# Tiles that begin at byte 128 of a 256-byte line, later state halves and a newly planned order, in an attention and feed-forward kernel

## The chip, the cores and the metric

The kernel runs on one core of a Trainium2 chip. The metric is the device time of one launch in microseconds, taken as the median of three runs. The engines are named as in the profile: PE multiplies matrices, DVE is the vector engine, ACT the scalar engine, POOL the third elementwise engine, SP a queue that only issues DMAs here.

## The reference

`x` holds 8 batches of 8 heads with 512 rows of 64 numbers, `state` 32 rows for each batch and head. The rows of `x` attend to the state, the state's rows attend to `x`, both results are put together to 544 rows of 512 numbers for each batch, and a feed-forward layer with a squared ReLU follows (512 to 2048 to 512).

```python
scores  = scale * x @ state^T;  a  = softmax(scores)    # 512 x 32 for each head
xread   = a @ state
scores2 = scale * state @ x^T;  a2 = softmax(scores2)   # 32 x 512 for each head
sread   = a2 @ x
rows = concat(xread, sread)                             # 544 rows of 512 for each batch
h = rows @ w_in;  r = maximum(h, 0);  out = (r * r) @ w_out
```

## The kernel before

**Precision.** Results have to be as good as fp32, while fp32r operands keep fewer bits. So every operand of the large products is split into a high and a low part (`split`, L379): ACT casts the high part (L384), and DVE or POOL subtracts it from the value for the low part (L389). A product is then three matmuls: high by high, low by high, high by low.

**Products.** The matrix `state · w_in`, called z, is computed once for each group of four batches. For the first four batches `z_part` (L537) computes it while the weights come in, stores it to DRAM (`zd`), and `z_fetch` loads it again batch by batch (`z_raw`), which is then split to `z_hi` and `z_lo`. For the later four, `z_halves` (L461) loads the state's halves into `st_raw`, splits them into `st_hi` (ACT) and `st_lo` (POOL), `w_halves` splits pieces of `w_in` (`wz`) and `z_heads` (L500) multiplies the two.

**Units.** The feed-forward part consists of 144 units: for each of 8 batches and each of 16 chunks of 128 columns of `w_in`, and 16 more for the state's rows. A unit is "up" (L879: six matmuls of 128x512 into `ph`, from `a` and z), ReLU on ACT (L885), a square on DVE or ACT (L893, L891), the split of the result into `g_hi` and `g_lo`, and "down" (L915: twelve matmuls into four `po` banks, from `g_hi`, `g_lo` and the `w_out` chunk's `wo_hi`, `wo_lo`). The batch 0 is done in two parts, chunks 0 to 5, and 6 to 15 after batch 1.

**Weights.** They arrive as 64-bit words. `singles` makes fp32 of a chunk: a guard multiply on ACT (L402), the top bits on DVE (L411) or ACT (L409), and two DVE operations (L416, L422). For `w_out` the result `wof` is then split into `wo_hi` and `wo_lo`.

**Attention.** `scores` computes the score products of a batch and head group and their exponentials `e`; `read` (L784) normalizes them (`e` times `s`, L797), transposes them on PE (`pt`, L802), splits them into `e_hl` (ACT, DVE), splits the rows of `x` into `xn_hl` (ACT, POOL), and multiplies (`pr`, L820). `both` (L833) sums the parts up, and POOL places them (L846).

**What sets the order.** Nothing is scheduled by hand. The class `Planner` (L47 to L257) simulates the engines with a cost for each operation (`pe`, `act`, `dve`, `dve2`, `gps`, L260 to L277) and picks for the engine that is free first the ready operation that is due first. A due time comes from the unit an operation serves, and the table `SHIFTS` moves it for the nth tile of a name. The flag `both` marks a DVE operation that the plan reckons as if it ran only after the POOL operation in progress. While the plan has nothing for PE at the start, it puts small matmuls there (`keep_busy`, L937: four matmuls `idle` each). The planned order is then the order of the instructions of each engine; a queue runs its own in that order. `FIRST` and `STEP` (L325) are the planned lengths of the first and of the later units.

`Buf` (L20) makes the tiles when the plan is known. SBUF tiles of one tag lie side by side, in the order in which the tags first occur; so a small tag moves all that lie behind it.

Of the kernel before, what the change touches and what calls it, by code (L numbers as in the profile page):

```python
# [19 lines left out]
class Buf:  # L20


    def __init__(self, pool, shape, dtype, name, tag, bufs, hot=False):
        self.make = lambda: pool.tile(shape, dtype, name=name, tag=tag, bufs=bufs)
        self.tag, self.bufs, self.hot = tag, bufs, hot
        self.name = name.rstrip("0123456789")
        self.t, self.users = None, []
# [19 lines left out]
class Planner:  # L47
# [5 lines left out]
    SLACKS = (2.5,)  # L53
    EARLY = 150.0
    SHIFTS = {
        ("g_lo", 1): (-9.6, 0.0),
        ("nm", 1): (7.3, -0.01),
        ("nm", 2): (6.9, 0.0),
        ("pa", 1): (9.8, -0.29),
        ("ph", 2): (-1.4, 0.38),  # L60
        ("po", 1): (-3.2, 0.28),
        ("po", 5): (8.2, 0.0),
        ("po", 8): (-2.0, 0.0),
        ("po", 14): (-4.0, 0.0),
        ("po", 17): (8.9, 0.18),
        ("po", 19): (-6.0, 0.02),
        ("pr", 1): (3.6, 0.0),
        ("pz", 1): (-3.2, 0.0),
        ("s", 2): (-3.3, 0.3),
        ("spill", 1): (-6.6, 0.0),  # L70
        ("wi", 1): (3.9, 0.0),
        ("wo", 1): (2.7, 0.0),
        ("wof", 1): (12.4, -0.2),
        ("z_hi", 1): (7.7, 0.0),
    }

    def __init__(self):
# [89 lines left out]
    def plan(self, scale):  # L167
        for o in self.ops:
            o.due, o.begin = self.time(o.want), self.time(o.start)
            o.left, o.ready, o.end = o.before, 0.0, None  # L170
        for o in reversed(self.ops):
            cost = o.engs[0][1] + o.lat + scale * o.slack + (o.size / self.RATE + o.land if o.size else 0.0)
            for s_ in o.succ:
                o.due = min(o.due, s_.due - cost)
            if o.next is not None:
                o.due = min(o.due, o.next.due)
            if o.hold is not None:
                o.begin = max(o.begin, o.due - o.hold)
        for o in self.ops:
            if o.due < self.EARLY and o.kind in self.SHIFTS:  # L180
                more, slope = self.SHIFTS[o.kind]
                o.due += more + slope * max(o.due, -30.0)
        free, slots, pending, wait, taken, cands = {}, {}, {}, {}, set(), {}
        queue = pool_end = 0.0
        for o in self.ops:
            for k in o.bufs:
                pending[k] = len(k.users)
                slots.setdefault(k.tag, [0.0] * k.bufs)

        def offer(o):  # L190
            for e, _ in o.engs:
                cands.setdefault(e, {})[o] = None

        for o in self.ops:
            if not o.left:
                offer(o)
        log = []
        left = sum(o.until > 1e17 for o in self.ops)
        while left:
            best = self.choose(cands, free, slots, taken, True) or self.choose(cands, free, slots, taken, False)  # L200
            assert best is not None, "no operation can begin"
            t, e, o = best
            cost = dict(o.engs)[e]
            for f, _ in o.engs:
                del cands[f][o]
            for k in o.bufs:
                if k not in taken:
                    slots[k.tag].remove(min(slots[k.tag]))
                    taken.add(k)
                    if k.hot:  # L210
                        for u in k.users:
                            u.due = min(u.due, t + 2.0)
            end = t + cost
            if e == "POOL":
                pool_end = end
            elif o.both and e == "DVE":
                end = max(end, pool_end + cost)
            free[e] = end
            if o.size:
                queue = max(queue, end) + o.size / self.RATE  # L220
                o.end = queue + o.land
            else:
                o.end = end + o.lat
            log.append((t, end, e, o))
            left -= o.until > 1e17
            for k in o.bufs:
                pending[k] -= 1
                wait[k] = max(wait.get(k, 0.0), o.end)
                if not pending[k]:
                    slots[k.tag].append(wait[k])  # L230
            for s_ in o.succ:
                s_.left -= 1
                s_.ready = max(s_.ready, end if e == "PE" == s_.engs[0][0] else o.end)
                if not s_.left:
                    offer(s_)
            if o.next is not None:
                o.next.left -= 1
                o.next.ready = max(o.next.ready, t)
                if not o.next.left:
                    offer(o.next)  # L240
        return log
# [22 lines left out]
def act(n, more=0.0):  # L264
    return ("ACT", 0.05 + more + n / 1200)
# [8 lines left out]


def gps(n):
    return ("POOL", 0.15 + n / 450)  # L277


@with_exitstack  # L280
def memory_attention_then_relu2_ffn(
# [40 lines left out]
    WARM = 88  # L322
    COLD = 8
    PARTS = [(0, 0, 6), (1, 0, NFC), (0, 6, NFC)] + [(b, 0, NFC) for b in (*range(2, B - 1), B, B - 1)]
    START, FIRST, STEP = 8.0, (3.5,), 4.4  # L325

    const = ctx.enter_context(tc.tile_pool(name="const", bufs=1))
    sb = ctx.enter_context(tc.tile_pool(name="sb", bufs=2))
# [64 lines left out]
    def singles(out_f, words, r, w):  # L393
# [5 lines left out]
        n = 512  # L399
        high_r, low_r = [(k, 1) for k in r], [(k, 0) for k in r]  # L400
        op(
            act(n, 0.08), lambda e: nc.scalar.activation(  # L402
                high().bitcast(F32), high().bitcast(F32), AF.Copy, scale=GUARD),
            r=high_r, w=high_r,
        )
# [5 lines left out]
                nc.vector.tensor_scalar(  # L411
                    out=bits(), in0=top(), scalar1=1 / 32, scalar2=-15.5 / 32, op0=ALU.mult, op1=ALU.add)

        op([dve(n), act(n, 0.08)], top_bits, r=low_r, w=w)
        op(
            dve(n), lambda e: nc.vector.scalar_tensor_tensor(  # L416
                out=bits(), in0=high(), scalar=3, in1=bits(),
# [43 lines left out]
    def z_halves():  # L461

        raw = tile_([P, H, GB * N], F32, "st_raw", "raw")
        high, low = (tile_([P, H, GB * N], F32R, n, "raw") for n in ("st_hi", "st_lo"))
        src = stT.rearrange("d (h b n) -> d h b n", h=H, b=B)[:, :, GB:, :]
        flat = lambda t, j: t.t.rearrange("p h m -> p (h m)")[:, j * S:(j + 1) * S]
        for i in range(2):
            load(
                lambda i=i: raw.t[i * D:(i + 1) * D].rearrange("d h (b n) -> d h b n", b=GB),
                lambda: src, 256, w=[(raw, i)], issue=1.0,  # L470
            )
        for j in range(2):
            split(
                lambda j=j: flat(high, j), lambda j=j: flat(low, j), lambda j=j: flat(raw, j), S,
                [(raw, i) for i in range(2)], [(high, j)], [(low, j)], engs=[gps(S)], chain="w1",
            )
        halves[:] = [high, low]
# [306 lines left out]
    def read(b, g, due, begin=0.0):  # L784
# [9 lines left out]
            nc.vector.reciprocal(s2.t, s2.t)  # L794

        op(("DVE", 0.3), invert, r=[s2], w=[s2], begin=begin)
        op(dve2(S), lambda e: nc.vector.tensor_scalar_mul(e2.t, e2.t, s2.t), r=[e2, s2], w=[e2])  # L797
        pt = tile_([P, NT, P], F32, "pt", "px")

        def turn(e):  # L800
# [48 lines left out]
                        in1=low.t[i * N:(i + 1) * N, q, i * D:(i + 1) * D],  # L849
                    )  # L850

        op(("POOL", 1.5), place, r=[both, low], w=[("sr", b, g)], due=due)


    def wo_tile(fc):
# [294 lines left out]
```

## Time and profile before

| | before |
|---|---|
| median of 3 runs | 683.01 us (682.32 to 683.97) |
| the profiled execution | 685.25 us, span 683.5 us |
[...]
| PE busy | 673.6 us (99%) |
| DVE, ACT, POOL busy | 433.7, 411.2 and 166.4 us |
| DMA | 79.80 MB, mean 117 GB/s |

The table of busy times says how much of the span each engine worked. A row of the timeline gives the start, the length, the engine, the line, the operation and its tiles; in brackets stands how long the engine had been idle before it, and what ended that. An operation's length overlaps the next one's start by up to a tenth of a microsecond, and a matmul's by more.

### The profile page before, as it was taken

How to read it: one execution, taken by the hardware profiler on the slowest of the kernel's cores; microseconds unless marked ns; L12 is line 12 of the kernel's file. 1: busy time of each engine (PE TensorE's matmuls, PEld its weight loads, DVE VectorE, ACT ScalarE, POOL GpSimd, SP SyncE). 2: the span in 40 equal slices, each digit the busy share in tenths (PEclk: the TensorE clock that was granted, in tenths of full speed). 3: DMA queues.
4: the chain of work that ended last, by engine and by line, in shares of the span. 5: the costliest groups of instructions: out<-in, count | busy, mean ns of one | idle time of the engine just before them, and what ended most of it. 6: DMA issues, size and time to landing. Idle time of an engine off the chain costs nothing.

```text
span 683.5 us, 9676 instructions
## 1 busy us (share of the span) xinstructions
PE 673.6 (99%) x3260; PEld 544.5 (80%) x3260; DVE 433.7 (63%) x717; ACT 411.2 (60%) x782; POOL 166.4 (24%) x183
## 2 busy tenths in 40 slices
PE   8999998999999999999999999999999999999997
PEld 7777776888888877888888888888888788988886
DVE  6999988457574588553954486347746855543333
ACT  5999776465486688576843584357656654443331
POOL 1010005114152354134500451035244640000000
PEclk9999999999999999999999999999999999999999
DMA  9998983231152343334221322113222201012101
GB/s 311 340 321 271 322 283 135 93 127 63 32 185 112 119 144 110 140 116 133 77 96 32 97 88 98 31 66 106 95 91 93 77 17 63 1 31 62 32 0 61
DMA packets 51681, 79.80 MB, mean 117 GB/s; under 512 B 7088, under 2 KB 34096, under 8 KB 51632
## 3 DMA queue, kind: packets, MB, share of 16 engines
q1 hardware_dynamic: 46544, 61.76, 27.6%
q10 hardware_dynamic: 5088, 17.44, 6.5%
q8 instruction: 25, 0.41, 0.2%
q14 instruction: 24, 0.20, 0.1%
HBM read 52.43 MB, written 26.74 MB: 116 GB/s over the span
## 4 chain that ended last, share of the span: by engine, by line
PE 79%; ACT 6%; DVE 6%; DMA 5%; issue 2%; POOL 1%; SPq 1%; ACTq 0%; DVEq 0%; POOLq 0%
PE po L915 46%; PE ph L879 25%; PE pr L820 2%; PE pz L500 2%; DMA w_raw<-w_in 2%; PE pq L690 1%; DMA z_raw<-zd 1%; DMA wo_raw<-w_out 1%; ACT z_stage L520 1%; PE pt L802 1%; DVE z_lo L389 1%; PE idle L942 1%; PE pz L537 1%; DMA zd<-z_stage 1%; DVE g_lo L389 1%
## 5 line engine op out<-in xcount | busy, mean ns | idle before, releaser
L915 PE MATMUL po<-wo_hi,g_hi 128*128 128x512 f32 x544 | 215.1, 395 | 0.0
L915 PE MATMUL po<-wo_lo,g_hi 128*128 128x512 f32 x544 | 213.2, 392 | 0.0
L885 ACT ACTIVATE r<-ph 128x512 f32<-128x512 f32 (+1 forms) x144 | 82.7, 574 | 159.9 <-PE ph L879 157.7
L893 DVE TENSOR_TENSOR ph<-ph,r 128x512 f32<-128x512 f32 (+1 forms) x120 | 79.6, 664 | 147.2 <-ACT r L885 146.9
L915 PE MATMUL po<-wo_hi,g_lo 128*128 128x512 f32 x544 | 154.2, 394 | 0.0
L915 PEld LDWEIGHTS po<-wo_hi,g_hi 128*128 128x128 f32 x544 | 102.2, 188 | 24.7 <-issue 1.7
L389 DVE TENSOR_TENSOR g_lo<-ph,g_hi 128x512 fp32r<-128x512 f32 (+1 forms) x144 | 94.4, 656 | 41.7 <-ACT g_hi L384 35.5
L915 PEld LDWEIGHTS po<-wo_lo,g_hi 128*128 128x128 f32 x544 | 102.2, 188 | 22.1
L915 PEld LDWEIGHTS po<-wo_hi,g_lo 128*128 128x128 f32 x544 | 100.0, 188 | 21.3 <-DVE g_lo L389 0.4
L384 ACT CAST g_hi<-ph 128x512 fp32r<-128x512 f32 (+1 forms) x144 | 81.1, 563 | 41.4 <-DVE ph L893 29.0
L879 PE MATMUL ph<-a_hi,z_hi 128*128 128x512 f32 x256 | 81.4, 399 | 0.3 <-DVE g_lo L389 0.2
L879 PE MATMUL ph<-a_lo,z_hi 128*128 128x512 f32 x256 | 80.9, 396 | 0.2 <-POOL a_lo L389 0.2
L879 PE MATMUL ph<-a_hi,z_lo 128*128 128x512 f32 x256 | 80.4, 395 | 0.0
L389 POOL TENSOR_TENSOR xn_hl<-xn_raw,xn_hl 128x512 fp32r<-128x512 f32 x32 | 42.3, 1321 | 149.5 <-ACT xn_hl L384 147.3
L879 PEld LDWEIGHTS ph<-a_lo,z_hi 128*128 128x128 f32 x256 | 48.2, 188 | 12.2 <-POOL a_lo L389 0.7
L879 PEld LDWEIGHTS ph<-a_hi,z_lo 128*128 128x128 f32 x256 | 48.1, 188 | 11.2
L879 PEld LDWEIGHTS ph<-a_hi,z_hi 128*128 128x128 f32 x256 | 46.7, 188 | 12.4 <-DVE g_lo L389 1.5
L389 DVE TENSOR_TENSOR z_lo<-z_raw,z_hi 128x512 fp32r<-128x512 f32 x63 | 47.9, 760 | 3.3 <-ACT z_hi L384 3.0
L389 POOL TENSOR_TENSOR xt_hl<-xt_raw,xt_hl 128x512 fp32r<-128x512 f32 x24 | 31.4, 1308 | 67.9 <-ACT xt_hl L384 66.6
L384 ACT CAST z_hi<-z_raw 128x512 fp32r<-128x512 f32 x63 | 38.9, 618 | 2.2 <-PE ph L879 1.5
L389 POOL TENSOR_TENSOR wz<-wi,wz 64x512 fp32r<-64x512 f32 x15 | 20.7, 1380 | 39.4 <-DVE wz L389 22.8
L749 POOL TENSOR_TENSOR q<-q,s 128x512 f32<-128x512 f32 x14 | 15.6, 1115 | 57.0 <-DVE s L744 44.4
(140 smaller groups left out, 795.6 us busy)
## 6 DMA issues: line engine op xcount, KB each, us to landing
w_raw<-w_in SPq DMA_DIRECT2D x16, 512.0 KB, 6.4
wo_raw<-w_out SPq DMA_DIRECT2D x16, 512.0 KB, 5.5
zd<-z_stage ACTq DMA_DIRECT2D x16, 512.0 KB, 5.0
xn_raw<-xn SPq DMA_DIRECT2D x16, 512.0 KB, 3.6
zq<-zq_stage ACTq DMA_DIRECT2D x16, 512.0 KB, 2.9
z_raw<-zq SPq DMA_DIRECT2D x128, 64.0 KB, 2.4
z_raw<-zd SPq DMA_DIRECT2D x124, 64.0 KB, 2.4
xt_raw<-xT SPq DMA_DIRECT2D x15, 512.0 KB, 3.6
```

Source lines behind the costliest of these rows:

```text
L384: act(n, 0.03 if both else 0.0), lambda e: nc.scalar.copy(out=hi(), in_=src()),
L389: lambda e: ENGINE[e].tensor_sub(out=lo(), in0=src(), in1=hi().bitcast(F32)),
L500: nc.tensor.matmul(pz.t, lhsT=halves[j].t[:, g * HG + 2 * q + i, :], rhs=m.t[:, i].rearrange("p c f -> p (c f)"), start=j == 0, stop=j == 1,)
L520: act(512), lambda e, i=i: nc.scalar.copy(out=part(i), in_=pz[i].t),
L537: nc.tensor.matmul(pz[i].t[:, q, :], lhsT=st[0].t[own, cc, :], rhs=wi[own, k * FPC:(k + 1) * FPC, cc, :], start=True, stop=True,)
L690: nc.tensor.matmul(pq.t, lhsT=sp_hl[:, g, q].rearrange("p i n -> p (i n)"), rhs=hl.t[:, i], start=i == 0, stop=i == 1,)
L749: two_source(S, b), lambda e: ENGINE[e].tensor_mul(out=q1.t, in0=q1.t, in1=s1.t.broadcast_to([P, NJ, N])),
L820: nc.tensor.matmul(pr.t[:, q].rearrange("p i c -> p (i c)"), lhsT=eh.t[:, t, q].rearrange("p i n -> p (i n)"), rhs=hl.t[:, t].rearrange("p ...
L879: nc.tensor.matmul(ph.t[:, :width], lhsT=w, rhs=v, start=j == 0, stop=j == len(pairs_) - 1)
L885: act(width), lambda e: nc.scalar.activation(rl.t[:, :width], ph.t[:, :width], AF.Relu),
L893: nc.vector.tensor_mul(out=ph.t[:, :width], in0=ph.t[:, :width], in1=rl.t[:, :width])
L915: nc.tensor.matmul(po[t].t, lhsT=(g[0], g[0], g[1])[j].t[:, t * P:(t + 1) * P], rhs=wo[k][j % 2][:, i, :], start=first and j == 0, stop=la ...
```

## The change

Four things change. First, `Buf` gives four small tags more columns (`nm2`, `m1`, `s1`: 32 columns, `s2`: 16), which moves all tiles behind them: before, most of these (`e2`, `q1`, `z_hi`, `z_lo`, `z_stage`, `a_hi`, `a_lo`, `wof`, `z_raw`, `r`, `g_hi`, `g_lo`, `os_`, `both`, `low`, `at`) begin at byte 64 or 192 of a 256-byte line, afterwards all begin at byte 128, where the weights, `x` and the `raw` tiles began already. Second, the loads of the state's halves may not begin before the time of batch 2. Third, the planner's costs and its rule for DVE and POOL are changed: a POOL operation is now also reckoned as if it ran only after a marked DVE operation in progress, the top bits (L411) and the multiply of `e` (L797) are marked too, and some costs differ (of `gps`, of the guard and top bits, of the placing; `FIRST`, the planned length of the first units, is 4.4 for 3.5). Fourth, the table `SHIFTS` has other entries (30 for 19).

```diff
+    LINE = {"nm2": 32, "m1": 32, "s1": 32, "s2": 16}
...
-        self.make = lambda: pool.tile(shape, dtype, name=name, tag=tag, bufs=bufs)
+        cols = max(shape[1], self.LINE.get(tag, 0))
+        self.make = lambda: pool.tile([shape[0], cols, *shape[2:]], dtype, name=name, tag=tag, bufs=bufs)[:, :shape[1]]
...
     SHIFTS = {
-        ("g_lo", 1): (-9.6, 0.0),
...
+        ("e", 1): (-5.0, 0.09),
...
             if e == "POOL":
-                pool_end = end
+                end = pool_end = max(end, dve_end + cost)
             elif o.both and e == "DVE":
-                end = max(end, pool_end + cost)
+                end = dve_end = max(end, pool_end + cost)
...
 def gps(n):
-    return ("POOL", 0.15 + n / 450)
+    return ("POOL", 0.2 + n / 440)
...
-    START, FIRST, STEP = 8.0, (3.5,), 4.4
+    START, FIRST, STEP = 8.0, (4.4,), 4.4
...
-            act(n, 0.08), lambda e: nc.scalar.activation(
+            act(n, 0.1), lambda e: nc.scalar.activation(
...
-        op([dve(n), act(n, 0.08)], top_bits, r=low_r, w=w)
+        op([("DVE", 0.36), act(n, 0.1)], top_bits, r=low_r, w=w, both=True)
...
-                lambda: src, 256, w=[(raw, i)], issue=1.0,
+                lambda: src, 256, w=[(raw, i)], issue=1.0, begin=At(begins[2] + 0),
...
-        op(dve2(S), lambda e: nc.vector.tensor_scalar_mul(e2.t, e2.t, s2.t), r=[e2, s2], w=[e2])
+        op(
+            dve2(S), lambda e: nc.vector.tensor_scalar_mul(e2.t, e2.t, s2.t), r=[e2, s2], w=[e2],
+            both=True,
+        )
...
-        op(("POOL", 1.5), place, r=[both, low], w=[("sr", b, g)], due=due)
+        op(("POOL", 1.42), place, r=[both, low], w=[("sr", b, g)], due=due)
```

Three places show what this does to the order; the lines of the changed kernel are 12 to 15 higher (L401 there is L389 here, L810 is L797). The first is POOL's beginning, the first reads of `x` (`xn_hl`) and the low parts of the state's halves (`st_lo`). Before:

```order
L749 TENSOR_TENSOR q_724<-q_724,s_741 128x512
L389 TENSOR_TENSOR xn_hl<-xn_raw,xn_hl 128x4x128
L389 TENSOR_TENSOR st_lo<-st_raw,st_hi 128x512
L389 TENSOR_TENSOR xn_hl<-xn_raw,xn_hl 128x4x128
L389 TENSOR_TENSOR st_lo<-st_raw,st_hi 128x512
L389 TENSOR_TENSOR xn_hl<-xn_raw,xn_hl 128x4x128
L846 TENSOR_TENSOR sr_80<-both,low 32x64 x4
```

Afterwards, further down in POOL's order, behind the second batch's `q` and ahead of the first `wz`:

```order
L761 TENSOR_TENSOR q_1852<-q_1852,s_1912 128x512
L401 TENSOR_TENSOR a_lo<-at,a_hi 128x512 x2
L401 TENSOR_TENSOR xn_hl<-xn_raw,xn_hl 128x4x128 x2
L401 TENSOR_TENSOR st_lo<-st_raw,st_hi 128x512 x2
L861 TENSOR_TENSOR sr_80<-both,low 32x64 x4
L401 TENSOR_TENSOR wz<-wi,wz 64x512 x5
```

The two `st_lo` have left the first reads and stand behind the reads of the third batch. The second place is DVE's order at the read in which `e` is multiplied for the sixth batch (near 530 us in the trace of before). Before:

```order
L725 STREAM_TRANSPOSE q_5452<-st 128x512
L728 TENSOR_REDUCE m_5461<-q_5452 128x16
L833 TENSOR_REDUCE both<-pr 128x256
L793 TENSOR_SCALAR s_5464<-s_5464 128x1
L794 RECIPROCAL s_5464<-s_5464 128x1
L389 TENSOR_TENSOR g_lo<-ph,g_hi 128x512
L797 TENSOR_SCALAR e_5463<-e_5463,s_5464 128x512
L739 TENSOR_REDUCE s_5498<-q_5452 128x16
L893 TENSOR_TENSOR ph<-ph,r 128x512
L389 TENSOR_TENSOR e_hl<-pt,e_hl 128x8x64
```

Afterwards:

```order
L737 STREAM_TRANSPOSE q_5471<-st 128x512
L740 TENSOR_REDUCE m_5475<-q_5471 128x16
L805 TENSOR_SCALAR s_5478<-s_5478 128x1
L806 RECIPROCAL s_5478<-s_5478 128x1
L848 TENSOR_REDUCE both<-pr 128x256
L810 TENSOR_SCALAR e_5477<-e_5477,s_5478 128x512
L401 TENSOR_TENSOR g_lo<-ph,g_hi 128x512
L401 TENSOR_TENSOR z_lo<-z_raw,z_hi 128x512
L908 TENSOR_TENSOR ph<-ph,r 128x512
L401 TENSOR_TENSOR e_hl<-pt,e_hl 128x8x64
```

The multiply of `e` stands one operation earlier, ahead of `g_lo`. The third place is DVE's order between the low parts of the fifth and the sixth chunk of `w_out`, which share the tile `wo_lo_88`. Before:

```order
L389 TENSOR_TENSOR wo_lo_88<-wof,wo_hi_87 128x512
L422 SCALAR_TENSOR_TENSOR wof<-wo_raw,wof 128x512
L389 TENSOR_TENSOR z_lo<-z_raw,z_hi 128x512
L893 TENSOR_TENSOR ph<-ph,r 128x512
L389 TENSOR_TENSOR wo_lo_88<-wof,wo_hi_87 128x512
```

Afterwards, the last twelve operations up to the second of the two:

```order
L428 SCALAR_TENSOR_TENSOR wi<-w_raw,wi 128x512
L401 TENSOR_TENSOR g_lo<-ph,g_hi 128x512
L401 TENSOR_TENSOR a_lo<-pa,a_hi 128x512
L401 TENSOR_TENSOR z_lo<-z_raw,z_hi 128x512
L428 SCALAR_TENSOR_TENSOR wof<-wo_raw,wof 128x512
L434 SCALAR_TENSOR_TENSOR wi<-w_raw,wi 128x512
L434 SCALAR_TENSOR_TENSOR wof<-wo_raw,wof 128x512
L401 TENSOR_TENSOR z_lo<-z_raw,z_hi 128x512
L428 SCALAR_TENSOR_TENSOR wi<-w_raw,wi 128x512
L401 TENSOR_TENSOR g_lo<-ph,g_hi 128x512
L434 SCALAR_TENSOR_TENSOR wi<-w_raw,wi 128x512
L401 TENSOR_TENSOR wo_lo_88<-wof,wo_hi_87 128x512
```

Twelve operations stand between the two low parts where there were three, and the conversions of `w_in` have moved ahead of the second. Before PE's first "up" there are 152 matmuls `idle` where there were 164.

## Rows read from the trace of the kernel before

**Rows 1.** The page, busy time, share of the span and instructions of each engine.
```profile
PE 673.6 (99%) x3260; PEld 544.5 (80%) x3260; DVE 433.7 (63%) x717; ACT 411.2 (60%) x782; POOL 166.4 (24%) x183
```

**Rows 2.** The waits of PE: us in total, times, longest us.
```profile
PE pr L820 <- DVE e_hl L389: 1.8, 1, 1.8
PE pt L802 <- DVE e L797: 1.1, 1, 1.1
...
PE ph L879 <- POOL a_lo L389: 0.2, 1, 0.2
...
PE pz L500 <- ACT zq_stage L509: 0.2, 1, 0.2
...
PE pr L820 <- POOL xn_hl L389: 0.2, 1, 0.2
```

**Rows 3.** Busy time in stretches: PE, PEld, DVE, ACT, POOL, clock, DMA share, GB/s.
```profile
40.00:60.00 20.00, 20.00 (x100) 15.21 (x99) 19.29 (x34) 19.21 (x38) 2.51 (x2) 1.00 0.96 289
...
100.00:120.00 20.00, 18.18 (x91) 13.94 (x91) 16.14 (x21) 12.62 (x24) 9.00 (x9) 1.00 0.40 133
```

**Rows 4.** PE's timeline at the head: start, length, operation, and count.
```profile
11.60 3.74 PE L942 MATMUL idle<-warm 128*128 128x128 bf16 x64
15.26 1.13 PE L537 MATMUL pz<-wi,st_z 64*128 64x256 f32 x8
```

**Rows 5.** The timeline of POOL at 106 to 112 us.
```profile
106.59 1.63 POOL L389 TENSOR_TENSOR st_lo<-st_raw,st_hi 128x512 fp32r<-128x512 f32 x1 [45.15 <-ACT g_hi L384]
...
109.61 1.74 POOL L389 TENSOR_TENSOR st_lo<-st_raw,st_hi 128x512 fp32r<-128x512 f32 x1
```

**Rows 6.** The timeline of DVE at 107 to 113 us.
```profile
107.09 1.41 DVE L411 TENSOR_SCALAR wof<-wo_raw 128x512 int32<-128x512 uint8 x1
108.42 0.68 DVE L389 TENSOR_TENSOR g_lo<-ph,g_hi 128x512 fp32r<-128x512 f32 x1
...
110.12 1.78 DVE L416 SCALAR_TENSOR_TENSOR wof<-wo_raw,wof 128x512 int32<-128x512 int32 x1
...
112.55 1.79 DVE L389 TENSOR_TENSOR z_lo<-z_raw,z_hi 128x512 fp32r<-128x512 f32 x1
```

**Rows 7.** The timeline of PE where `pr` waits.
```profile
116.27 0.71 PE L820 MATMUL pr<-xn_hl,e_hl 128*128 128x256 f32 x4 [1.78 <-DVE e_hl L389]
```

**Rows 8.** The timeline at 530 us: DVE, POOL, PE.
```profile
530.66 1.51 DVE L797 TENSOR_SCALAR e<-e,s 128x512 f32<-128x512 f32 x1
...
530.61 1.28 POOL L389 TENSOR_TENSOR xt_hl<-xt_raw,xt_hl 128x512 fp32r<-128x512 f32 x1 [0.18 <-ACT xt_hl L384]
...
532.32 0.63 PE L802 MATMUL pt<-ident,e 128*128 128x128 f32 x4 [1.07 <-DVE e L797]
```

**Rows 9.** Every multiply of `e`: duration ns min/median/max, first and last start.
```profile
L797 DVE TENSOR_SCALAR e<-e,s x16: 466/479/1511, 68.9 to 543.7; 128x512 f32<-128x512 f32 x16
```

**Rows 10.** Casts on ACT by tile: duration ns min/median/max.
```profile
L384 ACT CAST g_hi<-ph x144: 372/587/668, 29.5 to 675.5; 128x512 fp32r<-128x512 f32 x128, 128x256 fp32r<-128x256 f32 x16
...
L384 ACT CAST e_hl<-pt x16: 580/584/593, 95.0 to 547.9; 128x512 fp32r<-128x512 f32 x16
```

**Rows 11.** The chain of waits in two stretches: start, length, what.
```profile
171.91 1.41 PE ph L879 x6
173.32 2.75 PE po L915 x12
...
140.07 1.38 PE ph L879 x6
```

**Rows 12.** POOL's timeline at 193 us.
```profile
193.14 1.29 POOL L389 TENSOR_TENSOR xn_hl<-xn_raw,xn_hl 128x512 fp32r<-128x512 f32 x1 [15.82 <-ACT xn_hl L384]
```

**Rows 13.** SP's timeline where the state's halves are issued.
```profile
97.42 1.26 SPq L430 DMA_DIRECT2D st_raw<-stT  x2
```

**Rows 14.** The sixth chunk of `w_out`: its low part on DVE, and PE's use.
```profile
52.69 0.68 DVE L389 TENSOR_TENSOR wo_lo<-wof,wo_hi 128x512 fp32r<-128x512 f32 x1
...
58.37 0.39 PE L915 MATMUL po<-wo_lo,g_hi 128*128 128x512 f32 x1
```

More of the change, by code (lines that the diff above doesn't have):

```diff
@@ L55 @@
     SHIFTS = {
-        ("g_lo", 1): (-9.6, 0.0),
[L57 to L70, printed above, removed]
-        ("wi", 1): (3.9, 0.0),
-        ("wo", 1): (2.7, 0.0),
-        ("wof", 1): (12.4, -0.2),
-        ("z_hi", 1): (7.7, 0.0),
+        ("e", 1): (-5.0, 0.09),
+        ("e", 2): (-8.4, -0.08),
+        ("g_hi", 1): (-0.3, 0.0),
+        ("pa", 1): (-1.0, 0.0),
+        ("po", 1): (6.4, 0.46),
+        ("po", 2): (2.5, -0.02),
+        ("po", 5): (7.2, 0.0),
+        ("po", 7): (8.1, 0.0),
+        ("po", 10): (4.7, -0.07),
+        ("po", 12): (3.4, 0.0),
+        ("po", 15): (-2.9, 0.08),
+        ("po", 17): (6.4, 0.53),
+        ("po", 20): (1.1, 0.0),
+        ("po", 23): (11.5, -0.03),
+        ("po", 27): (-3.0, -0.25),
+        ("pq", 1): (16.2, -0.27),
+        ("pr", 1): (6.9, 0.04),
+        ("pz", 1): (-5.8, 0.0),
+        ("s", 2): (-5.2, 0.0),
+        ("sT", 1): (-10.0, -0.07),
+        ("st_raw", 1): (-6.6, 0.32),
+        ("w_raw", 1): (-0.8, 0.0),
+        ("wi", 1): (3.9, 0.0),
+        ("wi", 3): (-6.2, 0.01),
+        ("wo_raw", 1): (10.0, 0.0),
+        ("wof", 2): (2.2, 0.0),
+        ("z_hi", 1): (2.9, 0.18),
+        ("z_stage", 1): (5.7, 0.0),
     }
@@ L183, in plan @@
         free, slots, pending, wait, taken, cands = {}, {}, {}, {}, set(), {}
-        queue = pool_end = 0.0
+        queue = pool_end = dve_end = 0.0
         for o in self.ops:
```

## The prediction

> **What bounds the kernel now.** I read the busy times first. [...] The list of PE's waits [rows 2] names two that matter, 1.8 us for `e_hl` and 1.1 us for the multiply of `e`, and three of 0.2 us. The table of stretches then tells where. From 40 to 60 us DVE and ACT are nearly full (19.29 and 19.21 of 20) and the DMAs move all the time (0.96), and still PE is busy for 20.00 of 20 us. In the stretch 100:120 it loses 1.82 us, with 9.00 us of POOL beside it, while the DMAs have time to spare [rows 3]. Last I read the timelines at the two waits. At 116.27 us `pr` has waited 1.78 us for `e_hl` [rows 7]. Just before, DVE's operations on operands in SBUF are long: 1.41, 1.78 and 1.79 us, where such an operation takes 0.68 alone [rows 6, 14]. POOL runs `st_lo` for 1.63 and 1.74 us at the same time [rows 5], against 1.29 for one of the same size alone [rows 12]. The two engines hold each other up. At 530 us the multiply of `e` takes 1.51 us beside POOL's `xt_hl`, where its median is 0.479 us, and PE waits 1.07 us [rows 8, 9].
>
> **The change, term by term.** All terms are of the profiled execution of 685.25 us. The median is 683.01, 2.24 lower, and I take the difference from before to after to be the same for both.
>
> 1. *Fewer fillers at the head, -0.7 us.* Twelve of the `idle` matmuls fall away ahead of the first "up", and PE's real work ahead of it is the same. Sixty-four take 3.74 us, 0.058 each [rows 4], and the next operation there, `pz`, starts without a wait of its own, so PE's filling sets the pace of the head. 12 × 0.058 = 0.7. If the weights or the first `a` set it, the fillers become a wait and nothing is gained. Bounds: -0.9 to 0.
>
> 2. *The wait of `pr`, -1.8 us.* The three DVE operations of [rows 6] exceed 0.68 by 0.73 + 1.10 + 1.11 = 2.9 us, more than the wait of 1.78. In the new order both `st_lo` have left this place. Moreover DVE has 6 operations fewer ahead of this `e_hl` (four of them squares that ACT now does, five top bits of `w_out` fewer and four of `w_in` more), and PE has 8 `po` and 6 `ph` matmuls more ahead of this `pr`, 8 × 0.23 + 6 × 0.23 = 3.2 us by [rows 11] (2.75 us for 12 and 1.41 for 6). Late by 1.8, early by 2.9 and by 3.2: the wait should go whole, even if POOL's `xn_hl`, which stays, stretches one operation. What is late next is the first read, whose `pr` has come nearer to the beginning: ahead of it PE has 24 `po`, 6 `ph` and 8 `pz` matmuls fewer, and DVE only 4 operations fewer. It had no wait before, and how near it was no row tells. Bounds: -1.78 to 0.
>
> 3. *The wait of `pt`, -1.1 us.* The multiply stands one operation, 0.6 us, earlier on DVE, and the plan now reckons that POOL holds it up; were it still stretched to 1.51 us, PE would wait 1.07 - 0.6 = 0.5 us. Bounds: -1.07 to 0 (the stretch may as well strike one of the other 15).
>
> 4. *The three small waits, -0.3 us.* They sum to 0.6 [rows 2]. All three come of an order that has been redrawn; I take half. Bounds: -0.6 to 0.
>
> 5. *Where the tiles begin, 0.* If the byte within a line mattered to ACT or DVE it would show already: the cast to `g_hi`, which begins at byte 64, takes 587 ns, and the cast to `e_hl`, at 128, takes 584, both from PSUM [rows 10]. For PE the tiles are mixed: the weights of "down" begin at 128 and its `g` at 64, both operands of "up" at 64. A matmul of "down" takes 2.75 / 12 = 0.229 us, one of "up" 1.41 / 6 = 0.235, but elsewhere, with the same tiles, 1.38 / 6 = 0.230 [rows 11]. So the slower pace does not follow from the byte alone, and I take nothing. If it does go with the byte, 128 units gain 0.03 us each, 3.8 us; the other way I allow 1 us, which is what a third of "up" units falling from 1.38 to 1.41 costs (43 × 0.03 = 1.3).
>
> 6. *The state's halves later, 0.* SP needs 1.26 us for the two issues [rows 13]; they move from behind the weights to the stores of the first part of batch 0, past four stores and beside the `z_raw` fetches. POOL had been idle for 15.82 us ahead of 193.14 [rows 12], which is about where the two `st_lo` go. DVE does mostly `g_lo` and squares there, whose one input is in PSUM: such a `g_lo` took 0.68 us while POOL ran [rows 6]. If each `st_lo` still stretches an operation that PE waits for, by the 1.1 us of [rows 6], it is 2.2 us at most, and PE does not wait in that stretch by any row of [rows 2]. Bounds: 0 to 2.2.
>
> 7. *New waits, +0.5 us.* The old order had 3.7 us of waits after the head; the new one reckons with the mutual hold of DVE and POOL that both large waits came of, but its cost of POOL's 512 columns (0.2 + 512/440 = 1.36) lies further from the 1.28 to 1.29 of [rows 8, 12] than the old one (1.29), so plan and run will still differ. I allow two waits of the small kind. Bounds: 0 to 5 (rival C).
>
> Sum: -0.7 - 1.8 - 1.1 - 0.3 + 0 + 0 + 0.5 = -3.4, so 683.0 - 3.4 = **679.7 us**.
>
> [...]
>
> **Rivals.**
>
> A, *the matmuls of "up" speed up with the byte*: term 5 at its end, -3.8 more, 675.9 us. For it: the operands of "up" begin at 64, those of the faster "down" partly at 128, and only "up" has the two paces. Against it: the faster pace occurs with the old bytes too.
>
> B, *the waits only move*: the change does what it says at the two places, but the first read or another read of `x` becomes late in their place, because every read follows the same steps and the new order brings PE to the first one sooner than DVE. Then terms 2 to 4 give back what they save, only the fillers stay: 683.0 - 0.7 = 682.3, within 681.6 and 684.4. For it: at 40 to 60 us DVE and ACT are full, so what is moved forward there pushes something else back [rows 3].
>
> C, *PE waits for the sixth chunk of `w_out`*, the slower one. In the trace its low part is ready at 52.69 + 0.68 = 53.4 us and PE's first use is at 58.37, 5.0 us later [rows 14]. In the new order DVE has 13 operations more ahead of it: nine of full size at a pitch of 0.6, two top bits at 0.4, two small ones at 0.15, 6.5 us. PE has 12 `ph` matmuls (2.8 us) and a `pz` pair (1.1) [rows 4, 11] more ahead of the use, less the fillers (0.7). The margin is 5.0 - 6.5 + 2.8 + 1.1 - 0.7 = 1.7 us. From a delay of 1.7 us on PE waits. Up to 3.4 us of wait the time is still below the old; a delay of 6.5 us (a DVE stretched four times more by 1.1, or a chunk that arrives late, since the DMAs are at 0.96) makes a wait of 4.8 us, and 679.7 + 4.8 = 684.5. The typical time of this rival is 685.5. Against it: ACT takes over top bits of `w_out` and squares of units, so DVE has less left to do in the whole stage.
>
> **How the numbers follow.** A measurement of this kernel tells 0.2%, 1.4 us, from no change; faster is below 681.6, slower above 684.4. The forecast (678.0 to 681.6, all waits gone or all but 2 us) has a chance of 0.58, A 0.10, B or a small wait at C's place 0.18, C in full 0.14. That makes faster 0.68, same 0.18, slower 0.14. The range goes from A's end, 676.0, to 684.2, where the small waits end: it leaves out C in full (0.14) and what of A lies below 676.0 (0.04). The forecast's own range is 678.0 to 681.6.
>
> **What the changed kernel's profile would show.** Term 1: the first "up" starts 0.7 us earlier, at about 24.5 us. Terms 2 and 3: no wait of `pr` for `e_hl` and of `pt` for `e` above 0.5 us in the list of PE's waits; DVE's operations at the second read at 0.68 us; the first read's `pr` without a wait. Term 5: a "down" of 12 at 2.75 us and an "up" of 6 at 1.38 to 1.41, in the same mix; if A holds, all at 1.38 or less. Term 6: `st_lo` near 180 to 195 us, at 1.3 us each, and no wait of PE near it. Term 7 and C: a wait of PE `po` for `wo_lo` on DVE between 50 and 60 us would make the forecast wrong, as would a list of PE's waits that sums to over 3 us.

## The result, and the profile after

The changed kernel takes 676.74 us in the median of six runs (675.67 to 679.17). Runs of the kernel before on the same chips, three more among them, have a median of 684.16; the ratio is 0.9877, with a 95% interval of 0.9853 to 0.9901. That is faster by 1.2%, some 8.4 us, where the prediction had 3.4 us. (The two medians themselves lie 7.4 us apart.) The direction was right and the size was not; 676.74 lies in the range, near its lower end, where rival A stood, but terms of the sum were wrong in opposite directions.

The profiled execution of the changed kernel took 678.21 us, its span 676.4, 7.1 less than before. Its busy times, against [rows 1]:

```profile
PE 666.0 (98%) x3248; PEld 546.4 (81%) x3248; DVE 424.4 (63%) x711; ACT 415.5 (61%) x790; POOL 162.8 (24%) x181
```

PE is busy for 7.6 us less, though its products are the same. The list of PE's waits after, against [rows 2] (us in total, times, longest us):

```profile
PE ph L894 <- DVE g_lo L401: 1.9, 1, 1.9
PE idle L957 <- DVE warm L366: 1.0, 1, 1.0
PE pz L512 <- ACT zq_stage L521: 0.9, 2, 0.7
PE sT L729 <- DVE q L744: 0.9, 1, 0.9
PE ph L894 <- DVE z_lo L401: 0.7, 1, 0.7
PE po L930 <- ACT g_hi L396: 0.6, 1, 0.6
PE pa L770 <- DVE q L761: 0.2, 1, 0.2
```

The two large waits of before are gone, `pr` for `e_hl` and `pt` for `e`. Others are there instead, and the list is no shorter: 5.1 us without the `idle` one, where the list of before, with the lines that [rows 2] leave out, has 4.9. So the waits are not where the gain comes from. The chain of waits late in the run, where PE waits for nothing, shows where it comes from. First after, then before:

```profile
618.06 2.72 PE po L930 x12
620.78 1.36 PE ph L894 x6
622.14 2.72 PE po L930 x12
```

```profile
619.95 2.75 PE po L915 x12
622.70 1.41 PE ph L879 x6
624.11 2.75 PE po L915 x12
```

A unit takes 622.14 - 618.06 = 4.08 us after and 624.11 - 619.95 = 4.16 us before. Here an "up" is 0.05 us shorter and a "down" 0.03. This unit is one of the slower ones of before, so it can't stand for all. Over the whole trace, the mean distance from one start to the next (of those between 200 and 260 ns) falls from 232.8 to 227.5 ns in the 768 matmuls of "up" and from 230.0 to 227.7 ns in the 1631 recorded ones of "down": 4.1 and 3.8 us, some 8 us together. PE's matmuls run faster; the experiments show that the tiles' places do it. That is term 5, which I had put at nothing.

Part of it is given back in the first 100 us. Stretches of 20 us, after (PE, PEld, DVE, ACT, POOL, clock, DMA share, GB/s), against [rows 3]:

```profile
40.00:60.00 20.00, 19.02 (x92) 13.80 (x91) 17.77 (x33) 18.03 (x35) 3.82 (x3) 1.00 0.75 247
60.00:80.00 20.00, 18.06 (x83) 12.65 (x82) 17.06 (x33) 15.24 (x31) 0.00 (x0) 0.91 0.96 333
80.00:100.00 20.00, 20.00 (x96) 15.65 (x95) 17.04 (x28) 17.88 (x34) 0.00 (x0) 1.00 0.89 301
100.00:120.00 20.00, 20.00 (x101) 15.90 (x99) 15.10 (x26) 15.89 (x31) 4.86 (x6) 1.00 0.30 103
```

The hole at 100 to 120 is closed (20.00 for 18.18), and a new one has opened at 60 to 80, with a granted clock of 0.91, where the kernel before had 1.00. DVE there, and PE:

```profile
72.17 0.69 DVE L948 COPY os__987<-po 128x512 f32<-128x512 f32 x1 [1.94 <-DMA part<-os__932]
72.78 0.42 DVE L423 TENSOR_SCALAR wi<-w_raw 128x512 int32<-128x512 uint8 x1
73.11 0.69 DVE L401 TENSOR_TENSOR g_lo<-ph,g_hi 128x512 fp32r<-128x512 f32 x1
```

```profile
73.85 0.73 PE L894 MATMUL ph<-a_hi,z_hi 128*128 128x512 f32 x2 [1.94 <-DVE g_lo L401]
...
75.67 0.63 PE L930 MATMUL po<-wo_hi,g_hi 128*128 128x512 f32 x1
76.10 0.63 PE L930 MATMUL po<-wo_lo,g_hi 128*128 128x512 f32 x1
76.66 1.96 PE L549 MATMUL pz<-wi,st_z 64*128 64x256 f32 x8
```

```profile
74.00:75.00 1.00, 1.00 (x5) 0.98 1.05 420
75.00:76.00 1.00, 1.00 (x4) 0.50 0.98 285
76.00:77.00 1.00, 1.00 (x4) 0.50 1.04 330
```

The first of the three is DVE's timeline: a copy into an output tile waits for a buffer that a store has not yet freed. The DMAs are busy to the full (1.0 in the last fence: PE busy, clock, DMA share, GB/s by the microsecond). `g_lo` is queued behind that copy, and PE stands for 1.94 us. Some 1.1 us after it has gone on, at 74.95 us, the granted clock falls to 0.50, until 78.4 us. Two `po` are then 0.43 us apart (75.67, 76.10) instead of 0.23, and `pz` takes 1.96 us instead of 1.13 [rows 4]; from 74.89 to 78.54 us the lower clock costs some 1.7 us. By 100 us the kernel before has started 156 `po` matmuls and the changed one 140. This fall is not in every execution: the mean granted clock is 0.997 in three of the six and 0.999 in the other three.

The transfers are not at their limit all the time before that. From 50 to 60 us the DMAs move for 0.56 of the time, where they did for 0.93; after, then before:

```profile
50.00:60.00 10.00, 9.88 (x51) 7.48 (x50) 8.99 (x17) 10.00 (x21) 1.38 (x2) 1.00 0.56 177
```

```profile
50.00:60.00 10.00, 10.00 (x51) 7.56 (x50) 9.54 (x16) 9.45 (x19) 0.00 (x0) 1.00 0.93 293
```

SP, which issues the loads in its own order, waits there for DVE's `z_lo`, 3.3 us at the longest. What is not moved then has to be moved later.

### The profile page after: what moved, and what is told of

The parts are those of the page before. It is cut to its first block, busy times and chain, and to the rows that moved or that the text cites. A ratio compares the mean times of both kernels' runs of the same rounds, so it can differ in the third digit from the quotient of the medians.

```text
span 676.4 us, 9648 instructions
## 1 busy us (share of the span) xinstructions
PE 666.0 (98%) x3248; PEld 546.4 (81%) x3248; DVE 424.4 (63%) x711; ACT 415.5 (61%) x790; POOL 162.8 (24%) x181
## 4 chain that ended last, share of the span: by engine, by line
PE 85%; ACT 5%; DMA 5%; DVE 3%; issue 1%; SPq 1%; POOL 0%; ACTq 0%; DVEq 0%
PE po L930 51%; PE ph L894 26%; PE pr L835 2%; DMA wo_raw<-w_out 2%; PE pz L512 2%; PE pq L702 2%; DMA w_raw<-w_in 1%; PE pt L817 1%; DMA zd<-z_stage 1%; PE pz L549 1%; DMA part<-os__932 1%; ACT wz L396 1%; SPq L442 1%; ACT z_stage L532 1%; ACT r L900 0%
## 5 line engine op out<-in xcount | busy, mean ns | idle before, releaser
L908 DVE TENSOR_TENSOR ph<-ph,r 128x512 f32<-128x512 f32 (+1 forms) x113 | 74.8, 662 | 147.3 <-ACT r L900 147.1
L401 DVE TENSOR_TENSOR g_lo<-ph,g_hi 128x512 fp32r<-128x512 f32 (+1 forms) x144 | 94.6, 657 | 42.9 <-ACT g_hi L396 34.4
L401 POOL TENSOR_TENSOR xn_hl<-xn_raw,xn_hl 128x512 fp32r<-128x512 f32 x32 | 42.0, 1313 | 244.0 <-ACT xn_hl L396 220.8
L401 DVE TENSOR_TENSOR z_lo<-z_raw,z_hi 128x512 fp32r<-128x512 f32 x63 | 49.0, 779 | 3.3 <-ACT z_hi L396 3.1
L401 POOL TENSOR_TENSOR xt_hl<-xt_raw,xt_hl 128x512 fp32r<-128x512 f32 x24 | 31.5, 1313 | 63.4 <-ACT xt_hl L396 61.8
L401 POOL TENSOR_TENSOR wz<-wi,wz 64x512 fp32r<-64x512 f32 x13 | 17.4, 1337 | 38.9 <-ACT wz L396 22.4
L396 ACT CAST xn_hl<-xn_raw 128x512 fp32r<-128x512 f32 x32 | 19.8, 619 | 8.7 <-PE pr L835 5.4
```

The lines of the kernel that those rows point to most:

```text
L396: act(n, 0.03 if both else 0.0), lambda e: nc.scalar.copy(out=hi(), in_=src()),
L401: lambda e: ENGINE[e].tensor_sub(out=lo(), in0=src(), in1=hi().bitcast(F32)),
L908: nc.vector.tensor_mul(out=ph.t[:, :width], in0=ph.t[:, :width], in1=rl.t[:, :width])
```

## The experiments

**Place and order apart.** The order of every engine's instructions does not depend on the four padded tags (the traces show the same order with and without them), so each half of the change can run without the other. The kernel before with the padding alone:

```diff
+    LINE = {"nm2": 32, "m1": 32, "s1": 32, "s2": 16}
...
+        cols = max(shape[1], self.LINE.get(tag, 0))
```

> The kernel before with the four padded tags alone: the order of every engine is that of before, only the bytes at which the tiles begin are those of after. Theory P (the place of the tiles sets PE's pace): in the trace of after an 'up' of six takes about 1.36 us and a 'down' of twelve 2.72, against 1.38 to 1.41 and 2.75 before; 128 x 0.05 + 144 x 0.03 = about 9 to 10 us less, so 683.0 - 9 = 674 us (ratio 0.987), with the waits of 1.8 us (pr) and 1.1 us (pt) still there. Theory O (the new order brings the gain, the pace follows from it): no change, ratio 0.998 to 1.002, 'up' at 1.38 to 1.41. Both in part: between.

The changed kernel with these lines taken out:

> The changed kernel without the padded tags: order of after, bytes of before. P: the pace of before comes back ('up' 1.38 to 1.41), 676.7 + 9 = 686 us, so 0.3% or more slower than before, since the order of after has its own new waits (1.9 us at 72 us with a lower granted clock behind it, 0.7 us at 38 and at 261 us). O: 676.7 us (ratio 0.988), 'up' at 1.36.

| kernel | tiles | order | ratio to before (95%) |
|---|---|---|---|
| e1_before_lines | after | before | 0.9917 (0.9882 to 0.9952) |
| e2_after_nolines | before | after | 0.9976 (0.9956 to 0.9996) |
| changed kernel | after | after | 0.9877 (0.9853 to 0.9901) |

The place alone brings 0.8%, 5.7 us, the order alone 0.24%, 1.6 us, and together they make 1.2%. Neither theory has it whole, but the place carries most, and the pace goes with the place and not with the order. The chain of waits of e1 (order of before), then of e2 (order of after):

```profile
615.90 2.72 PE po L917 x12
618.62 1.36 PE ph L881 x6
```

```profile
616.25 2.75 PE po L928 x12
619.00 1.41 PE ph L892 x6
```

In e1's trace "up" runs at 227.6 ns and "down" at 227.9, in e2's at 232.8 and 230.0, the means of after and of before. Summed from start to start, "up" and "down" take 6.5 us less in e1 than before; 5.1 us of that reach its span. The wait of 1.8 us for `e_hl` is still there, and the last load of a `w_out` chunk is issued at 94.0 us, as in the kernel before. Two small waits of before are longer (`g_lo` 1.1 us for 0.2, `z_stage` 0.8 for 0.2), but they scatter from trace to trace in this order (0.4 and 1.8 us in e5 below), so they can't be laid to the quicker PE. e2 came out better than I expected of it (0.9976, and not slower than before): it has the old pace but a shorter list of waits, 3.8 us for 4.9.

e2 also tells where the wait at 72 us comes from. It has that wait with the old pace: PE's list, DVE's copy, and the stretch (as in [rows 3]):

```profile
PE ph L892 <- DVE g_lo L399: 1.9, 1, 1.9
```

```profile
70.18 0.69 DVE L946 COPY os__987<-po 128x512 f32<-128x512 f32 x1 [1.93 <-DMA part<-os__932]
```

```profile
60.00:80.00 20.00, 18.13 (x90) 13.03 (x89) 16.44 (x33) 15.27 (x30) 0.00 (x0) 1.00 0.97 346
```

So this wait belongs to the new order and not to the quicker PE. The DMA share from 50 to 60 us is low in e2 too, 0.64. And the clock stayed at 1.00 although PE stood for 1.87 us.

**Which byte, or which pair.** A kernel that only multiplies, with each pair of places in turn:

```diff
+PLACES = [(s, m) for s in (0, 64, 128, 192) for m in (0, 64, 128, 192)] + [(32, 128), (128, 32), (16, 128), (128, 16)]
...
+    a, b = s // 4 + j * P, m // 4 + (j % 4) * 512
+    nc.tensor.matmul(acc, lhsT=st[:, a:a + P], rhs=mv[:, b:b + 512], start=j == 0, stop=j == 5)
```

> Leaves the whole computation out: PE multiplies zeros, 128x128 weights by 128x512, 48 matmuls for each pair of places, in sixes into two banks. Letters give the byte of a 256-byte line at which the weights (st) and the streamed operand (mv) begin: A 0, B 64, C 128, D 192, E 32, F 16. P: a pair with C for both runs at about 0.227 us a matmul, and B or D for one of the two operands or both at 0.230 to 0.235; A like C if the half line counts, slower if the byte 128 itself does. O: all pairs the same within 0.001 us.

The letters are those of the expectation: st is the weights' tile, mv the streamed one. Groups of its profile (line, operation, tiles, count, then busy us and mean ns):

```profile
L33 PE MATMUL stC_mvE<-mv,st 128*128 128x512 f32 x48 | 11.4, 396 | 0.0
L33 PE MATMUL stB_mvA<-mv,st 128*128 128x512 f32 x48 | 11.4, 394 | 0.0
L33 PE MATMUL stA_mvC<-mv,st 128*128 128x512 f32 x48 | 11.3, 395 | 0.0
L33 PE MATMUL stB_mvC<-mv,st 128*128 128x512 f32 x48 | 11.2, 392 | 0.0
L33 PE MATMUL stC_mvC<-mv,st 128*128 128x512 f32 x48 | 11.1, 390 | 0.0
L33 PE MATMUL stB_mvB<-mv,st 128*128 128x512 f32 x48 | 11.1, 389 | 0.0
L33 PE MATMUL stA_mvA<-mv,st 128*128 128x512 f32 x48 | 11.0, 389 | 0.0
```

The mean ns contain the modelled ends of the matmuls. The distance from one start to the next, in the mean of 47, tells it finer (one execution, zeros as operands):

| weights at | streamed at 0 | 64 | 128 | 192 |
|---|---|---|---|---|
| 0 | 226.7 ns | 229.3 | 232.5 | 233.3 |
| 64 | 233.3 | 227.1 | 229.3 | 232.5 |
| 128 | 232.2 | 233.6 | 227.6 | 229.2 |
| 192 | 229.1 | 232.2 | 233.3 | 227.6 |

The diagonal is fast. What counts is not the byte but the distance: 227 ns where weights and streamed operand begin at the same byte of the line, 229 where the streamed one begins 64 further on, 232 at 128 and 233 at 192. The means hold a settling at the beginning of a pair; from the 13th start on, each distance has one pace whatever the bytes: 226.7, 228.9, 232.4 and 233.4 ns. Places off the grid of 64 (16 or 32 against 128) give 233 to 234. So theory P was right that the place counts, and wrong on the byte: A with A is as fast as C with C.

Before, `z_hi` (the weights of "up") began at 192 and `a` at 64, a distance of 128; `z_lo` and `a` both at 64; `g` (the weights of "down") at 64 and the `w_out` tiles at 128, a distance of 64. After, all are at 128. To test the rule in the kernel itself, everything was moved to byte 64:

```diff
+    const.tile([P, 48], F32, name="pad_a")
     ident = const.tile([P, P], F32, name="ident")
```

> The changed kernel with everything 192 bytes further on, so all tiles begin at byte 64 instead of 128. R: same time as the changed kernel, ratio 0.988 to before, 'up' 1.36 and 'down' 2.72. C: the pace of before comes back, ratio 0.998.

The ratio is 0.9886 (0.9853 to 0.9918), that of the changed kernel, and the chain shows its pace:

```profile
617.45 1.36 PE ph L895 x6
618.81 2.72 PE po L931 x12
```

So byte 128 has no merit of its own.

**The two kinds of pairs apart.** In the order of before, `z_hi` alone was moved to where `a` is:

```diff
+    PAD = {"z_hi": [32, None], "s1": [32, None]}
...
+            if tag in self.PAD and not self.PAD[tag][1]:
+                self.PAD[tag][1] = pool.tile([128, self.PAD[tag][0]], F32, name="pad_" + tag, tag="pad_" + tag, bufs=1)
```

> The kernel before, order untouched, with z_hi moved by 128 bytes, so that both operands of every 'up' matmul begin at byte 64 of a line (z_hi began at 192, z_lo and a at 64). Theory R (PE is at its fastest when weights and streamed operand begin at the same byte of a 256-byte line, whatever it is): 'up' of six falls from 1.41 to about 1.36, 'down' of twelve stays at 2.75; 128 x 0.04 to 0.05 = 5 to 6 us less, of which newly shown waits may give back 1 to 3: ratio 0.992 to 0.997. Theory C (byte 128 itself is the fast one): no change, ratio 0.998 to 1.002.

and the `w_out` tiles alone to where `g` is:

```diff
+    const.tile([P, 48], F32, name="pad_a")
     wo = [
...
+    const.tile([P, 16], F32, name="pad_b")
```

> The kernel before, order untouched, with the w_out tiles moved from byte 128 to byte 64, where g begins. R: 'down' of twelve falls from 2.75 to about 2.72, 'up' stays at 1.38 to 1.41; 144 x 0.03 = 4 us less, less newly shown waits: ratio 0.994 to 0.998. C: the weights leave byte 128, so no gain, and a loss of up to 4 us if that is the fast byte: ratio 1.000 to 1.006.

The ratios are 0.9991 (0.9969 to 1.0012) and 0.9966 (0.9942 to 0.9991). The first misses what I expected and is not clear of no change, the second makes it in part. The chains, of e4 and of e5:

```profile
622.91 1.39 PE ph L885 x6
624.29 2.76 PE po L921 x12
```

```profile
622.79 1.40 PE ph L881 x6
624.19 2.73 PE po L917 x12
```

With its own pairs equal, "up" comes to 1.39 only, not to 1.36. The two halves sum to 0.4% where both together bring 0.8%. The single pairs had hinted at the reason: behind an unequal pair the equal ones needed five to ten matmuls to settle (the first starts of C with C are 229, 229, 233, 236, 224, 231, 236, 228, 233, 231 ns apart, then 226 to 227). The next run puts the kernel's own sequence of six and twelve on PE alone:

```diff
+MIXES = {"old": (192, 64, 64, 64, 128), "upeq": (64, 64, 64, 64, 128), "dneq": (192, 64, 64, 64, 64),
+         "alleq": (64, 64, 64, 64, 64), "new": (128, 128, 128, 128, 128)}
```

> Leaves the whole computation out: PE multiplies zeros in the kernel's own sequence, six matmuls of an 'up' and twelve of a 'down', twelve units for each mix of places. old: the bytes of before (z_hi 192, z_lo, a and g 64, w_out 128); upeq: the 'up' pairs equal, 'down' as before; dneq: the 'down' pairs equal, 'up' as before; alleq: all at 64; new: all at 128. The run of single pairs gave 227 ns where both begin at the same byte, 229 at a distance of 64, 232 to 233 at 128 and 192, and about ten matmuls until the pace had settled after a change. Theory S (an unequal pair disturbs the equal ones behind it): old about 18 x 231, alleq and new 18 x 227, while upeq and dneq win less than their pairs' share, upeq the least since only six equal ones stand in a row: 'up' in upeq at 230 to 232, 'down' in dneq at 228 to 229. Theory I (each matmul has its own pace): 'up' 227 in upeq and 'down' 227 in dneq.

| mix | "up", mean of 6 | "down", mean of 12 | a unit |
|---|---|---|---|
| old | 234.3 ns | 229.6 | 4.16 us |
| upeq | 231.5 | 229.8 | 4.15 |
| dneq | 233.6 | 227.1 | 4.13 |
| alleq | 226.7 | 226.7 | 4.08 |
| new | 226.9 | 226.9 | 4.08 |

Theory S holds: six equal pairs behind twelve unequal ones gain about a third of what they could (234.3 to 231.5, of 226.7), twelve behind six most of it (229.6 to 227.1). 128 units of this table give 10 us for both, 2 us for "up" alone and 4 us for "down" alone, beside the 0.6 and 2.3 us that e4 and e5 gained. The rows of old and new, 4.16 and 4.08, are the late units of the two kernels to the hundredth of a microsecond; over the whole kernel, with other matmuls between the units, it was some 8 us.

**The order's own part.** Only the later begin of the state's halves, in the kernel before:

```diff
-                lambda: src, 256, w=[(raw, i)], issue=1.0,
+                lambda: src, 256, w=[(raw, i)], issue=1.0, begin=At(begins[2] + 0),
```

> The kernel before with the later begin of the state's halves alone, so the two st_lo leave the first reads. Term 2 of the prediction: the wait of pr for e_hl (1.8 us) goes, 683.0 - 1.8 = 681.2 us (ratio 0.997), and no wait of over 0.5 us comes in the first 120 us. Rival: the wait only moves to another read of the first 120 us, 683.0 us (ratio 1.000).

The ratio is 0.9989 (0.9974 to 1.0003): 0.8 us in the mean, less than half of what I expected, and not clear of no change. The wait of `pr` for `e_hl` is gone from the list, that of `pt` as well, and others stand there:

```profile
PE ph L879 <- DVE g_lo L389: 1.4, 2, 1.0
PE idle L942 <- DVE warm L354: 1.0, 1, 1.0
PE sq L652 <- DMA xt_raw<-xT: 0.8, 1, 0.8
PE pr L820 <- POOL xn_hl L389: 0.5, 2, 0.3
```

The step does what it says. Whether the waits only moved, as rival B has it, is not shown: the 0.8 us for `xt_raw` stands at 8.6 us, where before had 1.0 us for `st`, and the wait for `g_lo` at 65.6 us (1.0 us for 0.2) is one of those that scatter.

**What gives the pace back at the start.** The wait at 72 us was behind a store. The changed kernel with a fourth buffer for output rows, in the same order, was run twice, the second time beside the changed kernel itself:

```diff
-        self.make = lambda: pool.tile([shape[0], cols, *shape[2:]], dtype, name=name, tag=tag, bufs=bufs)[:, :shape[1]]
+        self.make = lambda: pool.tile([shape[0], cols, *shape[2:]], dtype, name=name, tag=tag, bufs=bufs + (tag == "os_"))[:, :shape[1]]
```

> The changed kernel in its own order, with a fourth buffer for the output rows (os_) that the planner does not know of. If the new wait at 72 us (DVE and ACT idle until a store frees an os_ buffer, PE 1.9 us without g_lo, then a granted clock of 0.5 for about 3 us) comes of that store: it goes, 1.9 + about 1.5 us less, 673.3 us where the changed kernel took 676.7 (ratio 0.983). Rival: the stretch is held by the DMAs anyhow and PE waits as long for the next chunk of weights, ratio 0.988.

> The changed kernel once more, beside its form with a fourth buffer for output rows: 676.7 us, ratio 0.988 to before; in its trace the wait of about 1.9 us for g_lo near 72 us.

> The changed kernel with the fourth buffer for output rows, again, for a direct comparison on one chip. [...] If the DMAs decide: the same within 0.5 us.

The ratios are 0.9863 (0.9834 to 0.9892) and then 0.9883 (0.9861 to 0.9905), with 0.9869 (0.9849 to 0.9889) for the changed kernel beside it. So nothing is gained. In the first of the two the wait at 72 us and the fall of the clock are gone (the mean granted clock is 0.999 or more in all eleven executions), and PE waits at another place, behind a DVE that waits for a chunk of `w_out`. DVE, then PE:

```profile
84.12 0.69 DVE L428 SCALAR_TENSOR_TENSOR wof<-wo_raw,wof 128x512 int32<-128x512 int32 x1 [2.49 <-ACT wo_raw L414]
```

```profile
87.27 0.72 PE L894 MATMUL ph<-a_hi,z_hi 128*128 128x512 f32 x2 [1.52 <-DVE g_lo L401]
```

That points to the transfers rather than to the one store. The last run adds to them, in the order of after:

```diff
+            if more:
+                ENGINE[e].dma_start(out=spare.bitcast(I32), in_=in_()[:, :DM])
...
-            w=[(raw, 0), (raw, 1)],
+            w=[(raw, 0), (raw, 1)], more=fc in (3, 4, 5, 6, 7, 8, 9, 10),
```

> The changed kernel with eight transfers of 256 KB more, each issued by SP behind one of the loads of w_out chunks 3 to 10, into a tile that nothing reads; the rest of the order is untouched. Theory D (the first 100 us of the changed kernel end when the weights have come in, and PE waits for them): 2.1 MB at some 330 GB/s are 6.3 us, and the time grows by 4 to 7 us, to a ratio of 0.994 to 0.998 to the kernel before. Rival: the DMAs have slack, and it grows by under 1.5 us (ratio 0.988 to 0.990).

The ratio is 0.9992 (0.9977 to 1.0007), where the changed kernel beside it had 0.9869: 685.76 for 676.36 us, 9.4 us more for 2.1 MB, more than I allowed. PE's longest wait, and ACT's before it:

```profile
104.27 0.94 PE L823 MATMUL pt<-ident,e 128*128 128x128 f32 x4 [4.64 <-ACT z_stage L538]
```

```profile
102.55 0.66 ACT L422 ACTIVATE wof<-wo_raw 128x512 int32<-128x512 uint8 x1 [4.51 <-DMA wo_raw<-w_out]
```

So the rival is out: the transfers of the changed kernel have no slack in the first 100 us, and PE waits for the weights, as theory D says, though more than it allowed. That the DMAs of the changed kernel move only 0.56 of the time from 50 to 60 us suggests that the issue order limits them as well as the rate (a share of 0.96 at 333 GB/s from 60 to 80 us); no run changes that order alone. The excess over 6.3 us has the size of the lower clock again (0.84 in the stretch 60:80, 0.91 in 100:120), which I have not separated.

## Why the prediction was right and wrong

**Term 5, the place of the tiles, is the step that failed.** I put 0 and it is some -8 us of pace. Two errors made it. First, I wrote that both operands of "up" begin at 64. `z_hi` began at 192; had I listed every tile of both operands, the two paces of "up" would have stood beside a distance of 128 and of 0. Second, I concluded from the 1.38 us at 140 us [rows 11], got "with the same tiles", that the place was no cause. The runs of single pairs and of mixes show that one pair's pace depends on the ones before it. The "up" at 140 us stands behind eight matmuls of "down", the one at 171.91 us behind twelve; I have not run that difference alone. A counterexample from one neighbourhood did not exclude the cause. The bound of -3.8 us, taken from "up" alone, is near what "up" gave (4.1 us); it lacks the 3.8 us of "down", whose 0.229 us I held for the floor, and 0.227 is possible. The casts on ACT [rows 10] were read rightly but tell nothing on PE, whose matmuls have two operands in SBUF.

**Rival A was the nearest to what happened**, at 675.9 us and a chance of 0.10. Its mechanism, that the byte itself is the cause, was wrong (e6), but the effect, and that it sits in the matmuls, was right. That its time comes out is luck: it had 3.8 us of pace and 3.4 us of order, and it was 8 us of pace, of which the first 100 us gave some back. Why 227 or 233 ns follow from the distance between the two operands' bytes, no run here shows.

**Term 7, new waits, was too small.** I took 0.5 us. The listed waits of after sum to 5.1 us, nearly all of them new, and the lower clock behind the longest costs 1.7. The place was not that of rival C. The longest wait comes of the new order (e2 has it too): DVE's copy stands ahead of `g_lo` and waits for a store while the transfers are at their limit (a DMA share of 1.00 from 72 to 74 us), and with a fourth buffer another wait for weights takes its place. The last `w_out` load is issued at 98.5 us (97.6 in the second trace, 95.2 in e2) where it was 94.0. I had read that PE was busy for 20.00 of 20 us at a DMA share of 0.96 and took it for cover; the new order leaves the DMAs idle for nearly half of 50 to 60 us (a share of 0.56 for 0.93), and the cover is gone; that the one follows from the other is argued, not run. I also read the list of before too short: it has five waits of 0.2 us and one of 1.0 us at the head (`sT` at 8.08 us), so 3.9 us stood after the head and not 3.7.

**Term 1 failed.** The first "up" starts at 25.22 us (24.78 in the second trace) and started at 25.15. The seven traces with the new order have it at 24.2 to 26.0 us, 25.0 in the mean. The twelve fillers are gone and nothing is gained: at 14.95 us `pz` is 0.3 us earlier than before, and at 20.05 us `sq` is 0.1 us later, behind a `pa` that waits for DVE.

**Terms 2 and 3 were right about the waits.** Both are gone, and DVE's operations at the second read take 0.68 us. One reading was off: the `z_lo` of 1.79 us ran beside POOL's `xn_hl` (from 112.08 us, 1.71 us), not beside `st_lo`, which had ended. One multiply of `e` still takes 1.51 us, but PE doesn't wait for it. As a saving of time the terms were too large: e3 takes the same two waits away and gains 0.1%, not clear of nothing, and the order as a whole gains 1.6 us (e2), where terms 1 to 4 and 7 had 3.4.

**Term 4** came out the other way: two of the three small waits are gone, that of `pz` has grown from 0.2 to 0.9 us in two pieces, and two of 0.6 and 0.7 us are new. **Term 6** was right in its size, 0: the two `st_lo` run from 198.4 us, a little later than I had said, at 1.29 and 1.74 us, and two `wz` of DVE beside them take 3.28 us together; PE's list has no wait for any of these.

In sum, in the profiled span, counted from each matmul's start to the next one's: "up" and "down" take 583.4 us before and 576.2 after, and some 0.8 us of the lower clock lie in the latter, so the pace is worth -8.1. With +0.2 of listed waits (5.1 for 4.9), +1.7 for the clock and -0.9 for all other matmuls that makes -7.1, as measured.

## What to carry to other kernels

Where PE is busy for 99% of the time, look at the distance between starts of matmuls before looking at waits: if the same shape has two paces (here 1.41 and 1.38 us for six), list the byte within a line at which both operands begin, and put weights and streamed operands at the same one (here 226.7 ns, where the other distances had 228.9 to 233.4), all of them, since a mixed sequence gained less than its share here ("up" came to 231.5 ns in upeq, to 226.7 in alleq). A stage in which PE is just covered while the transfers run near their limit (here 20.00 of 20 us at a DMA share of 0.96) is no free stage: a new order that leaves the DMAs idle early in it (0.56 of 50 to 60 us) may lack its cover later, which is argued here and not run, and behind the wait of 1.94 us that came here the granted clock was 0.50 for 3.4 us on top. Waits that are taken away need not count in full: in e3 waits of 1.8 and 1.1 us went, and the gain was 0.8 us, not clear of no change.

## What the runs showed of the hardware

- A matmul of 128x512 behind its own weights, both fp32r, starts 226.7 ns after the one before it where the operands begin at the same byte of a 256-byte line, once the pace has settled; 228.9 where the streamed one begins 64 bytes further on, 232.4 at 128 and 233.4 at 192 (one execution, zeros, the granted clock at 1.00). Six equal ones behind twelve unequal ones take 231.5 in the mean. In the kernel itself both moves, to byte 128 and to byte 64, give the same pace.
- With the transfers of the first 100 us made longer by 2.1 MB the kernel took 9.4 us more, more than the 6.3 us that they need at 330 GB/s, an estimate from the stretch 60:80.
- The granted clock fell from 1.00 to 0.50 at 74.95 us, 1.1 us after PE had stood for 1.94 us and gone on, and came back 3.4 us later. In the second trace of the changed kernel it fell at 72.9 us, while PE still stood (until 73.06 us):

```profile
72.00:73.00 1.00, 0.00 (x0) 0.94 0.92 296
```

In e6 PE stood for 1.68 us and the clock fell (0.996 in the mean of that execution); in e2 it stood for 1.87 us, in the kernel before for 1.78 us, and the clock stayed (1.00 from 60 to 80 and from 100 to 120 us). So the length of the wait alone did not decide it; what did is not shown.
